# Turning keys and probabilities on VectorE as 4-byte blocks in a decode attention kernel

## The chip, the core and the metric

The kernel runs on one core of a Trainium2 chip. A core has TensorE (PE, matrix products into PSUM), VectorE (DVE), ScalarE (ACT), GpSimd (POOL) and SyncE (SP, which here issues nearly all transfers), and 16 DMA engines that carry data between HBM and SBUF. The metric is the time of one execution on the device in microseconds. A profiled execution also has a span, the time from the first to the last recorded instruction.

## The reference

One decode step of a layer: the input is normalised, one branch is attention over the last 2048 positions of a key and value cache, the other a gated unit that ends in a gate; the result is `x + s * silu(b)`. Cut to what matters:

```python
B, Sq, D = 8, 1, 512
Hq, Hkv, Sk, Dh = 32, 8, 8192, 128
W = min(4096, max(256, Sk // 4))               # 2048
xn = _layernorm(x)
q = (xn @ wq).reshape(B, Sq, Hq, Dh)...
k = jnp.repeat(k_cache[:, :, Sk - W:, :], rep, axis=1)     # rep = 4
v = jnp.repeat(v_cache[:, :, Sk - W:, :], rep, axis=1)
p = _softmax(einsum("bhqd,bhkd->bhqk", q, k) * Dh ** -0.5)
s = einsum("bhqk,bhkd->bhqd", p, v)... @ wo
h = sigmoid(xn @ w_gate) * (xn @ w_up)         # F = 1792
return x + s * silu(h @ w_down)
```

All inputs are bf16. The two caches' windows are 32 MB each, so 64 of the 81 MB that the kernel reads.

## The kernel before, in words

A *tile* here is the pair (b, i): one of 8 batch rows and one of `NQ` = 2 groups of `G` = 4 key heads. Its keys and its values are one load of 2 MB each, `k_sb` and `v_sb`, with 128 partitions of 64 positions (`CT`) times 128 elements. Partition p holds 64 consecutive positions of head p // 32. There are 16 tiles.

Loads are listed in `todo` and issued in that order on SP (`pump`, L111): a load is issued when a buffer of its tag is free (`room`, 5 buffers of tag "k" and 4 of tag "v"), and a load that has to wait holds up all loads behind it. The order is the weights of the gated unit, wq, w_down, then keys with values three tiles behind (`AHEAD`), then the 32 rows per partition of wo in five loads of tag "k". `wd_part` (L185 to 200) holds the first `SD` = 2 of the 14 rows per partition of w_down, dealt to a few partitions by `SHARES` = ((0, 5, 4), (32, 4, 3)): partitions from 0 on, 4 x 5 of them with 4 shares each, and from 32 on, 4 x 4 with 3 each. `sel_part` and `hP_sb` bring the hidden values into the same order.

Keys come with positions on partitions, but the score product needs the head dimension there. `k_transposes` (L482) turns a quarter of a tile: 16 PE transposes of 128x128 (matmuls against `perm`) into PSUM, `kT_ps`, and one DVE copy of 2048 columns to SBUF, `kT_sb`. `scores` (L498) then makes four matmuls, one per head, each on 32 columns of PE; `qm_sb` is padded with zeros so that the heads of both tiles and all quarters of one batch row b add up in one PSUM tile `s_ps` of 128 rows and 512 columns.

Softmax is per batch row: `row_max` (DVE, 512 columns), `stat_rows` (a PE transpose, `top` and `neg` on DVE, which join the row maxima of the quarters), `spread_max` (a PE transpose back, an ACT copy `nb`, four exponentials on ACT that write the rows of each head into `p_buf`, where the places of the other heads were zeroed once by POOL). `p_transposes` (16 PE transposes against `turn_rows`, one DVE copy) makes `pT_sb`. `values` makes 64 matmuls per batch row in 32-column parts of PE, each 128x256; half of each result is unwanted, and `combine` (ACT, then DVE) picks with `own_col`. `normalise` (`heads`, `divide`) and `sums` divide by the sums of the exponentials into `oP_sb`.

The loop over b (L689) spreads these steps over 16 places by hand: in the time of row b's key transposes stand the softmax of b-1 and the values of b-2. There is no scheduler; the program order on each engine is the order of the code. After the loop (L716 to 745) the last two rows are interleaved by hand.

The end (L747 on): rows 0 to 19 of wo go into `part_ps`, an ACT copy gives `part`; `fin_ps` takes `part` by way of `sel_z` first and then rows 20 to 31; `prod` and `y_bf` on DVE; one store. The gate (`w_ps`, `b_ps`, `gg_sb`, L389 to 421) is computed before the loop.

Of the kernel before, what the change touches and what calls it, by code (L numbers as in the profile page):

```python
# [10 lines left out]
def kernel(  # L11
# [31 lines left out]
    CH = CU // 2  # L43
    NU = NQ * NJ
    NR = NU * rep
# [9 lines left out]

    padpool = ctx.enter_context(tc.tile_pool(name="padpool", bufs=1))
# [3 lines left out]
    ktpool = ctx.enter_context(tc.tile_pool(name="ktpool", bufs=3))  # L60
    ppool = ctx.enter_context(tc.tile_pool(name="ppool", bufs=2))
# [23 lines left out]
    room = {"k": 5, "v": 4, "d": 1}  # L85
# [85 lines left out]
    SD = 2  # L171
    SHARES = ((0, 5, 4), (Z, 4, 3))
# [40 lines left out]
    for t0, t1 in ((0, 12), (12, KS), (KS, 26), (26, 30), (30, RT)):  # L213
        want_rows("wo_sb", A_wo, "k", RT, t0, t1)

    pump()

    perm = consts.tile([P, P], bf16, name="perm")
    nc.gpsimd.tensor_copy(
        out=perm[:].rearrange("k (l p) -> k l p", l=G),  # L220
        in_=ident[:].rearrange("k (p l) -> k l p", l=G),
    )

# [34 lines left out]
    M0 = Z - rep  # L258
    qm_sb = work.tile([P, B, Hkv, M0 + Z], bf16, name="qm_sb")
    nc.gpsimd.memzero(qm_sb[:])  # L260
    p_buf = [work.tile([P, PG, G, CU], bf16, name=f"p_buf{i}") for i in range(2)]
    for t in p_buf:
        nc.gpsimd.memzero(t[:])
# [74 lines left out]
    JQ = NB  # L338
    q_ps = [ps_s.tile([P, rep * Dh], f32, name="q_ps", tag="s") for _ in range(2)]
    for kt in range(KT):  # L340
        for x in range(Hkv // JQ):
            for j in range(JQ):
                g = x * JQ + j
                nc.tensor.matmul(  # L344
                    q_ps[x][Z * j : Z * (j + 1), :],
                    lhsT=xnT_sb[:, kt, :],
                    rhs=weights[("wq_sb", kt)][:, g * rep * Dh : (g + 1) * rep * Dh],
                    start=(kt == 0),
                    stop=(kt == KT - 1),
                    tile_position=(0, Z * j),  # L350
                    skip_group_check=True,
                )
    q_bf = ktpool.tile([P, 2, rep, Dh], bf16, name="q_bf", tag="kT")
    qT_ps = ps_t.tile([P, 2, rep, P], bf16, name="qT_ps", tag="t")
    for x in range(Hkv // JQ):
        src = q_ps[x][:].rearrange("k (r d) -> k r d", r=rep)
        nc.scalar.copy(out=q_bf[:, x], in_=src)
    for x in range(Hkv // JQ):
        for r in range(rep):
            nc.tensor.transpose(  # L360
                out=qT_ps[:, x, r, :], in_=q_bf[:, x, r, :], identity=ident[:]
            )
        nc.vector.tensor_copy(  # L363
            out=qm_sb[:, :, x * JQ : (x + 1) * JQ, M0 : M0 + rep],
            in_=qT_ps[:, x].rearrange("d r (j z) -> d z j r", z=Z)[:, ::S],
        )

    free("k")
    free("k")

    down = [(hT_sb[:, t, :], weights[("wd_sb", t)]) for t in range(SD, FT)]
# [12 lines left out]
    for x in range(SX):  # L384
        top = max(p0 + 4 * a for p0, a, sx in SHARES if x < sx)
        down += [
            (hP_sb[:top, x, Z * r : Z * (r + 1)], d_part[:top, x, r, :])
            for r in range(SD)
        ]  # L389


    w_ps = ps_s.tile([P, D], f32, name="w_ps", tag="s")
    for t, (h, w) in enumerate(down):
        j = t % NB
        nc.tensor.matmul(
            w_ps[Z * j : Z * (j + 1), :],
            lhsT=h,
            rhs=w,
            start=(t < NB),
            stop=(t >= len(down) - NB),  # L400
            tile_position=(0, Z * j),
            skip_group_check=True,
        )
    w_sb = ktpool.tile([P, 2, 512], f32, name="w_sb", tag="kT")
    nc.scalar.copy(out=w_sb[:, 0], in_=w_ps[:])
    b_ps = ps_s.tile([P, P], f32, name="b_ps", tag="s")
    for j in range(NB):
        nc.tensor.matmul(
            b_ps[Z * j : Z * (j + 1), :],
            lhsT=sel_z,  # L410
            rhs=w_sb[:, 0, j * P : (j + 1) * P],
            start=True,
            stop=True,
            tile_position=(0, Z * j),
            skip_group_check=True,
        )
    sigb = work.tile([P, P], f32, name="sigb")
    nc.scalar.activation(out=sigb[:], in_=b_ps[:], func=AF.Sigmoid)
    free("v")
    gg_sb = work.tile([P, P], f32, name="gg_sb")  # L420
    nc.vector.tensor_tensor(out=gg_sb[:], in0=sigb[:], in1=b_ps[:], op=ALU.mult)

    Hh = G * rep
    turn_rows = consts.tile([P, P], bf16, name="turn_rows")
    sel_den = consts.tile([P, Hq], f32, name="sel_den")
    sel_out = consts.tile([P, 2, Hq], f32, name="sel_out")
    for i in range(NQ):
        nc.gpsimd.tensor_copy(
            out=turn_rows[:].rearrange("k (i j l r) -> k i j l r", i=NQ, j=NJ, l=G)[
                :, i  # L430
            ],
            in_=ident[:].rearrange("k (l j i r) -> k i j l r", i=NQ, j=NJ, l=G)[:, i],
        )
        nc.vector.reduce_sum(
            out=sel_den[:, i * Hh : (i + 1) * Hh].rearrange("k (l r) -> k l r", l=G),
            in_=ident_f[:].rearrange("k (l j i r) -> k i l r j", l=G, j=NJ, i=NQ)[:, i],
            axis=AX.X,
        )
    for e in range(2):
# [19 lines left out]
    sel_sum = consts.tile([P, Hq, NDQ], f32, name="sel_sum")  # L459
    nc.gpsimd.tensor_copy(  # L460
        out=sel_sum[:], in_=sel_den[:].unsqueeze(2).to_broadcast([P, Hq, NDQ])
    )


    o_ps = ps_o.tile([P, 2, 2 * Dh], f32, name="o_ps")
# [5 lines left out]
    kT_ps = {}  # L471
# [10 lines left out]
    def k_transposes(b, u, h):  # L482
        i, j = u // NJ, u % NJ
        k_sb = k_tiles[(b, i)]
        if h == 0:
            kT_ps[0] = ps_t.tile([P, CU, P], bf16, name="kT_ps", tag="t")
        for c in range(h * CH, (h + 1) * CH):
            nc.tensor.transpose(  # L488
                out=kT_ps[0][:, c, :], in_=k_sb[:, j * CU + c, :], identity=perm[:]
            )  # L490
        if h == 1:
            kT[(b, u)] = ktpool.tile([P, CU, P], bf16, name="kT_sb", tag="kT")
            nc.vector.tensor_copy(out=kT[(b, u)][:], in_=kT_ps.pop(0)[:])  # L493
        if j == NJ - 1 and h == 1:
            del k_tiles[(b, i)]
            free("k")

    def scores(b, u):  # L498
        i, j = u // NJ, u % NJ
        if u == 0:  # L500
            s_ps[b] = ps_s.tile([P, CU * PG], f32, name="s_ps", tag="s")
        t = kT.pop((b, u))
        o = M0 - rep * (j * NQ + i)
        for l in range(G):
            nc.tensor.matmul(  # L505
                s_ps[b][NR * l : NR * (l + 1), :],
                lhsT=qm_sb[:, b, i * G + l, o : o + Z],
                rhs=t[:, :, PG * l : PG * (l + 1)],
                start=(u == 0),
                stop=(u == NU - 1),  # L510
                tile_position=(0, NR * l),
                skip_group_check=True,
            )


    NH = NQ * rep

    def row_max(b):
        st[b] = small.tile([P, 1], f32, name="st")
        nc.vector.reduce_max(out=st[b][:], in_=s_ps[b][:], axis=AX.X)  # L520

    def stat_rows(b):
        nc.tensor.transpose(out=r_ps[b % 2], in_=st.pop(b)[:], identity=ident_f[:])
        top = small.tile([1, G, NH], f32, name="top")
        nc.vector.reduce_max(
            out=top[:],
            in_=r_ps[b % 2].rearrange("o (l j h) -> o l h j", l=G, j=NJ),
            axis=AX.X,
        )
        row[b] = small.tile([1, G, NJ, NH], f32, name="neg")  # L530
        nc.vector.tensor_scalar(
            out=row[b][:],
            in0=top[:].unsqueeze(2).to_broadcast([1, G, NJ, NH]),
            scalar1=-scale,
            scalar2=None,
            op0=ALU.mult,
        )

    def spread_max(b):
        nc.tensor.transpose(  # L540
            out=nb_ps[b % 2],
            in_=row.pop(b)[:].rearrange("o l j h -> o (l j h)"),
            identity=ident_f[0:1, 0:1],
        )
        nb = small.tile([P, 1], f32, name="nb")
        nc.scalar.copy(out=nb[:], in_=nb_ps[b % 2])  # L546

        s = s_ps.pop(b)
        if b % 2 == 0:
            sums_of[b // 2] = small.tile([P, 2], f32, name="sums")  # L550
        if b == B - 1:
# [37 lines left out]
    def p_copy(b, c0, c1, copy):  # L589
        copy(out=pT[b][:, c0:c1, :], in_=pT_ps[b][:, c0:c1, :])  # L590
        if c1 == CU:
            del pT_ps[b]
# [227 lines left out]
```

## Time and profile before

| | |
|---|---|
| time, median of 3 runs | 199.51 us (199.36 to 199.6) |
| profiled execution | 199.11 us, span 197.3 us |
| busy: PE / weight loads / DVE / ACT / POOL | 155.2 / 105.4 / 114.9 / 35.8 / 13.8 us |
| instructions | 4706, of them 2138 matmuls and 2138 weight loads |
| DMA | 81.32 MB in 6436 packets, mean 412 GB/s |
| granted TensorE clock, mean | 0.972 |
| key transposes on PE (1024) | 76.5 us |
| copies of the turned keys on DVE (64) | 78.2 us |

The page lists busy time per engine, then the span in 40 slices with a digit for the busy tenths, then DMA queues, then the chain of work that ended last, then groups of instructions: line, engine, operation, tiles written and read, shape, count, then busy time, mean of one in ns, then the idle time of the engine just before them and what ended it. In a table of stretches each row has the length, the busy time and count of each engine, granted clock, DMA share and GB/s. In a chain or a timeline each row starts with start and length in us. In the slices of a chosen stretch the stretch is again cut in 40.

### The profile page before, as it was taken

The numbers are of one execution on the slowest core, as the hardware profiler recorded it, in microseconds if no ns is written. First come the engines' busy times: TensorE is split into PE (matmuls) and PEld (weight loads), VectorE is DVE, ScalarE is ACT, GpSimd is POOL, SyncE is SP. The second block draws the span as 40 slices with busy tenths as digits, with TensorE's granted clock in tenths as the row PEclk, the third lists the DMA queues.
The fourth block names the chain that finished last, engine by engine and source line by source line (L and its number), as shares of the span: only waits on it lengthen the run. The fifth ranks groups of instructions, "written<-read, shape, count | busy, mean of one in ns | idle before, by whom it ended". The sixth has DMA issues, their size and how long they took to land.

```text
span 197.3 us, 4706 instructions
## 1 busy us (share of the span) xinstructions
PE 155.2 (79%) x2138; PEld 105.4 (53%) x2138; DVE 114.9 (58%) x144; ACT 35.8 (18%) x87; POOL 13.8 (7%) x32
## 2 busy tenths in 40 slices
PE   0073575999799996999798979796989797749763
PEld 0021124777586675667565746474658464538521
DVE  4624002889877574657794766476848664764311
ACT  0510210000900600060006001500050024032110
POOL 8960001000000000000000000000000000010000
PEclk9999999999999998899999999999999999999975
DMA  6999999999999999999999999999999999999980
GB/s 212 436 438 438 423 431 422 432 435 425 428 428 435 423 428 428 442 422 425 425 432 423 432 432 425 435 428 428 432 428 425 425 428 432 438 428 424 407 372 29
DMA packets 6436, 81.32 MB, mean 412 GB/s; under 512 B 777, under 2 KB 785, under 8 KB 1553
## 3 DMA queue, kind: packets, MB, share of 16 engines
q1 hardware_dynamic: 6237, 80.10, 95.3%
q10 hardware_dynamic: 180, 0.93, 1.4%
q8 instruction: 16, 0.26, 0.5%
q14 instruction: 3, 0.02, 0.0%
HBM read 81.02 MB, written 0.01 MB: 411 GB/s over the span
## 4 chain that ended last, share of the span: by engine, by line
DMA 75%; PE 20%; SPq 1%; DVE 1%; issue 0%; ACT 0%; DVEq 0%
DMA k_sb<-in_A_k_cache_dram 62%; PE kT_ps L488 11%; DMA wo_sb<-in_A_wo_dram 10%; PE o_ps L625 4%; DMA wg_sb<-in_B_w_gate_dram 3%; PE s_ps L505 3%; PE fin_ps L768 1%; PE pT_ps L599 1%; SPq L90 1%; DVE kT_sb L493 1%; PE part_ps L754 1%; ACT part L764 0%; SPq L100 0%; SPq L150 0%; DVE prod L783 0%
## 5 line engine op out<-in xcount | busy, mean ns | idle before, releaser
L493 DVE COPY kT_sb<-kT_ps 128x2048 bf16<-128x2048 bf16 x64 | 78.2, 1222 | 37.0 <-PE kT_ps L488 36.6
L488 PE MATMUL kT_ps<-perm,k_sb 128*128 128x128 bf16 x1024 | 76.5, 225 | 12.3 <-DMA k_sb<-in_A_k_cache_dram 12.2
L488 PEld LDWEIGHTS <-k_sb 128*128 128x128 bf16 x1024 | 60.5, 100 | 32.5 <-issue 16.3
L625 PE MATMUL o_ps<-v_sb,pT_sb 128*32 128x256 bf16 x512 | 38.7, 276 | 2.3 <-DVE pT_sb L590 2.3
L625 PEld LDWEIGHTS <-pT_sb 128*32 128x32 bf16 x512 | 21.6, 96 | 10.8 <-DVE pT_sb L590 2.7
L505 PE MATMUL s_ps<-kT_sb,qm_sb 128*32 128x512 bf16 x256 | 25.9, 393 | 1.4 <-DVE kT_sb L493 1.2
L573 ACT ACTIVATE p_buf<-s_ps,nb 32x512 bf16<-32x512 f32 x28 | 19.0, 679 | 0.5
L546 ACT COPY nb<-m_ps 128x1 f32<-128x1 f32 x8 | 1.3, 159 | 91.9 <-PE m_ps L540 91.9
L590 DVE COPY pT_sb<-pT_ps 128x2048 bf16<-128x2048 bf16 (+1 forms) x8 | 9.3, 1158 | 5.0 <-PE pT_ps L599 5.0
L505 PEld LDWEIGHTS <-qm_sb 128*32 128x32 bf16 x256 | 7.4, 93 | 8.3 <-issue 1.9
L599 PE MATMUL pT_ps<-turn_rows,p_buf 128*128 128x128 bf16 x128 | 9.9, 229 | 1.1 <-ACT p_buf L573 1.1
L569 POOL COPY p_buf<-e_sb 32x512 bf16<-32x512 bf16 x1 | 0.7, 667 | 143.1 <-ACT e_sb L553 143.1
L599 PEld LDWEIGHTS <-p_buf 128*128 128x128 bf16 x128 | 8.8, 150 | 3.0 <-issue 1.6
L641 ACT ACTIVATE o_odd<-o_ps,own_col 128x128 f32<-128x128 f32 x8 | 2.9, 367 | 29.6 <-PE o_ps L625 29.6
L248 PE MATMUL xnT_ps<-ident,xn_bf 8*128 8x8 bf16 x4 | 0.3, 174 | 10.1 <-DVE xn_bf L237 10.1
L344 PE MATMUL q_ps<-wq_sb,xnT_sb 128*32 128x512 bf16 x32 | 3.8, 625 | 5.7 <-DMA wq_sb<-in_A_wq_dram 5.7
L520 DVE TENSOR_REDUCE st<-s_ps 128x1 f32<-128x512 f32 x8 | 5.4, 680 | 0.5 <-PE s_ps L505 0.5
L248 PEld LDWEIGHTS <-xn_bf 8*128 8x128 bf16 x4 | 0.2, 114 | 10.1 <-DVE xn_bf L237 10.1
L344 PEld LDWEIGHTS <-xnT_sb 128*32 128x32 bf16 x32 | 1.3, 130 | 8.1 <-issue 8.1
L363 DVE COPY qm_sb<-qT_ps 128x128 bf16<-128x128 bf16 x2 | 0.6, 292 | 8.2 <-PE qT_ps L360 8.2
L674 DVE SCALAR_TENSOR_TENSOR own<-m_ps,inv,own_q 128x128 f32<-128x128 f32 x8 | 2.8, 347 | 4.2 <-PE m_ps L664 4.2
L573 ACT ACTIVATION_READ_ACCUMULATOR p_buf<-s_ps,nb 32x1 f32 x28 | 5.1, 184 | 0.0
(86 smaller groups left out, 76.5 us busy)
## 6 DMA issues: line engine op xcount, KB each, us to landing
k_sb<-in_A_k_cache_dram SPq DMA_DIRECT2D x16, 2048.0 KB, 31.2
v_sb<-in_A_v_cache_dram SPq DMA_DIRECT2D x16, 2048.0 KB, 27.3
wq_sb<-in_A_wq_dram SPq DMA_DIRECT2D x2, 2048.0 KB, 16.7
wu_sb<-in_B_w_up_dram SPq DMA_DIRECT2D x1, 1792.0 KB, 10.2
wd_sb<-in_B_w_down_dram SPq DMA_DIRECT2D x1, 1536.0 KB
wo_sb<-in_A_wo_dram SPq DMA_DIRECT2D x1, 1536.0 KB, 18.3
wo_sb<-in_A_wo_dram SPq DMA_DIRECT2D x1, 1024.0 KB
wg_sb<-in_B_w_gate_dram ACTq DMA_DIRECT2D x1, 896.0 KB
```

The lines of the kernel that those rows point to most:

```text
L90: q0.dma_start(out=t[:].rearrange("p c d -> p (c d)"), in_=cache[b, G * i : G * (i + 1), win0:Sk, :].rearrange("l (p c) d -> p l (c d)", c ...
L344: nc.tensor.matmul(q_ps[x][Z * j : Z * (j + 1), :], lhsT=xnT_sb[:, kt, :], rhs=weights[("wq_sb", kt)][:, g * rep * Dh : (g + 1) * rep * Dh ...
L488: nc.tensor.transpose(out=kT_ps[0][:, c, :], in_=k_sb[:, j * CU + c, :], identity=perm[:])
L493: nc.vector.tensor_copy(out=kT[(b, u)][:], in_=kT_ps.pop(0)[:])
L505: nc.tensor.matmul(s_ps[b][NR * l : NR * (l + 1), :], lhsT=qm_sb[:, b, i * G + l, o : o + Z], rhs=t[:, :, PG * l : PG * (l + 1)], start=(u ...
L520: nc.vector.reduce_max(out=st[b][:], in_=s_ps[b][:], axis=AX.X)
L573: nc.scalar.activation(out=p_buf[b % 2][rows, :, l, :], in_=s[rows, :].rearrange("k (c p) -> k p c", p=PG), func=AF.Exp, bias=nb[rows, :], ...
L590: copy(out=pT[b][:, c0:c1, :], in_=pT_ps[b][:, c0:c1, :])
L599: nc.tensor.transpose(out=pT_ps[b][:, c, :], in_=p_buf[b % 2][:, :, :, c].rearrange("k p l -> k (p l)"), identity=turn_rows[:],)
L625: nc.tensor.matmul(o_at[b][rows].rearrange("k (e d) -> k e d", e=2), lhsT=pT[b][:, c, rows], rhs=v[:, m, c], start=(c == 0), stop=(c == CU ...
L641: nc.scalar.mul(out=o_odd[:], in_=o_at[b][:, Dh:], mul=own_col[:, 1:2])
L674: nc.vector.scalar_tensor_tensor(out=own[:], in0=m_ps[:, b % 2, P : 2 * P].rearrange("p (q t) -> p q t", q=NDQ), scalar=inv[b // 2][:, b % ...
```

## The change

- Keys are turned on DVE. `turn_keys` issues one 32x32-block transpose over half a key tile, read as 4-byte words (two neighbouring bf16 elements are one word): 2048 words per partition, SBUF to SBUF. A block turn stays inside 32 partitions, that is, inside one head. The PE transposes, `perm`, `kT_ps` and the PSUM copies go.
- After such a turn each partition quadrant holds the 32 words of one head's elements, and the two elements of a word lie side by side. So `scores` makes, per half tile, eight matmuls of 512 columns with the full 128 columns of PE: two halves `e` of 16 positions, times four quarters `y` of the head dimension, whose key elements are read with a step of two. `qm_sb` is laid out anew for it (spread queries, 32 short matmuls, four moves on ACT and four on DVE). One further matmul per half with 4 contracted rows (`mask_rows`, `mask_cols`) adds minus a large number to the places where a row of one head meets the keys of another.
- Softmax is per tile (16 times) instead of per batch row (8 times): `row_max` over 1024 columns, and one exponential of 128x1024 for all heads; the masked places become zero by themselves. `p_buf` needs no zeroing.
- The probabilities are turned on DVE too, 512 words per partition (`turn_p`); `pT_sb` is read by `values` as weights with a step of two elements.
- `combine` is one DVE product; `heads` adds its two halves in two matmuls. `sums` takes two matmuls.
- The loop runs over the 16 tiles, staggered: the turn of t, the softmax of t-1, the turn of the probabilities of t-2, the values of t-4. The gate's end is placed behind the scores of the first tile.
- Key buffers 4 instead of 5, `pT_sb` buffers 3 instead of 2; the last wo load takes a buffer of tag "v".
- `SD` = 1 and `SHARES` = ((0, 5, 6), (32, 2, 1)): one row per partition of w_down instead of two is dealt out.
- At the end `sel_z` stands behind the fifth of the rows of wo that go into `fin_ps`, not ahead of the first.
- The PE's instruction list is 2031 rows instead of 4205, DVE's 134 instead of 107.

```diff
-    kpool = ctx.enter_context(tc.tile_pool(name="kpool", bufs=5))
+    kpool = ctx.enter_context(tc.tile_pool(name="kpool", bufs=4))
...
-    ppool = ctx.enter_context(tc.tile_pool(name="ppool", bufs=2))
+    ppool = ctx.enter_context(tc.tile_pool(name="ppool", bufs=3))
...
-    room = {"k": 5, "v": 4, "d": 1}
+    room = {"k": 4, "v": 4, "d": 1}
...
-    SD = 2
-    SHARES = ((0, 5, 4), (Z, 4, 3))
+    SD = 1
+    SHARES = ((0, 5, 6), (Z, 2, 1))
...
+    def turn_keys(t, m):
+        k_sb = k_tiles[order[t]]
+        kT[(t, m)] = ktpool.tile([P, NJE // NE, CM, PG, NE], bf16, name="kT_sb", tag="kT")
+        nc.vector.transpose(
+            out=kT[(t, m)][:].rearrange("k y c p e -> k c y (p e)").bitcast(f32),
+            in_=k_sb[:, CM * m : CM * (m + 1), :]
+            .rearrange("k c (y d) -> k c y d", y=NJE // NE).bitcast(f32),
+        )
...
+    def scores(t, m):
...
+        nc.tensor.matmul(
+            s_ps[t][:, m],
+            lhsT=mask_rows[:].rearrange("k x l r -> k (x l r)"),
+            rhs=mask_cols[:].rearrange("k c l -> k (c l)"),
+            start=True,
+            stop=False,
+        )
+        keys = kT.pop((t, m))
+        for e in range(2):
+            for y in range(NJE):
+                nc.tensor.matmul(
+                    s_ps[t][:, m],
+                    lhsT=qm_sb[i][:, y, b, GR * (1 - e) : GR * (1 - e) + P],
+                    rhs=keys[:, y // NE, CU * e : CU * (e + 1), :, y % NE],
+                    start=False,
+                    stop=(e == 1 and y == NJE - 1),
+                )
...
+    def turn_p(t):
+        pT[t] = ppool.tile([P, NM * CU // 2, NX, 2], bf16, name="pT_sb")
+        nc.vector.transpose(
+            out=pT[t][:].rearrange("k c x e -> k (c x e)").bitcast(f32),
+            in_=p_buf[t % 2][:].rearrange("k c p e -> k (c p e)").bitcast(f32),
+        )
...
+    for t in range(NT):
+        turn_keys(t, 0)
+        if t >= 1:
+            row_max(t - 1)
+        if t >= 2:
+            turn_p(t - 2)
+        if t >= LAG:
+            values(t - LAG)
+        if t >= 1:
+            stat_rows(t - 1)
+        turn_keys(t, 1)
+        scores(t, 0)
+        if t >= 1:
+            spread_max(t - 1)
+        scores(t, 1)
+        if t == 0:
+            gg_sb = gate()
+        if t >= LAG and t % 2 == 1:
+            combine((t - LAG) // 2)
+        if t >= 8 and t % 4 == 0:
+            normalise((t - 8) // 2, (t - 8) // 2 + 2)
+        if t >= 5 and t % 4 == 1:
+            sums((t - 5) // 4)
...
     for t in range(KS, RT):
-        if t == KS:
-            into_blocks(sel_z, part[:, 0, :], True, False)
-        into_blocks(oP_sb[:, t, :], weights[("wo_sb", t)], False, t == RT - 1)
+        into_blocks(oP_sb[:, t, :], weights[("wo_sb", t)], t == KS, t == RT - 1)
+        if t == KS + 4:
+            into_blocks(sel_z, part[:, 0, :], False, False)
```

More of the change, by code (lines that the diff above doesn't have):

```diff
@@ L383 @@
     nc.scalar.copy(out=hP_sb[:], in_=hP_ps[:])
[L384 to L425, printed above, removed]
[L426 to L438 removed]
+    sel_den = consts.tile([P, GR], f32, name="sel_den")
+    sel_out = consts.tile([P, 2, Hq], f32, name="sel_out")
+    nc.vector.reduce_sum(
+        out=sel_den[:],
+        in_=ident_f[:].rearrange("k (x h) -> k h x", h=GR),
+        axis=AX.X,
+    )
     for e in range(2):
```

458 lines of the change are left out of this document (224 added, 234 removed).

## The prediction

> **What bounds the kernel now.** I read the page's busy shares and slices first, then the DMA queues and the chain, then the table of stretches.
>
> ```profile
> PE 155.2 (79%) x2138; PEld 105.4 (53%) x2138; DVE 114.9 (58%) x144; ACT 35.8 (18%) x87; POOL 13.8 (7%) x32
> DMA  6999999999999999999999999999999999999980
> q8 instruction: 16, 0.26, 0.5%
> DMA k_sb<-in_A_k_cache_dram 62%; PE kT_ps L488 11%; DMA wo_sb<-in_A_wo_dram 10%; PE o_ps L625 4%; DMA wg_sb<-in_B_w_gate_dram 3%; PE s_ps L505 3%; PE fin_ps L768 1%; PE pT_ps L599 1%; SPq L90 1%; DVE kT_sb L493 1%; PE part_ps L754 1%; ACT part L764 0%; SPq L100 0%; SPq L150 0%; DVE prod L783 0%
> ```
>
> ```profile
> 0.00:32.00 32.00, 12.41 (x108) 4.34 (x108) 9.96 (x16) 5.71 (x9) 12.67 (x30) 1.00 0.95 399
> 86.00:125.00 39.00, 35.13 (x503) 24.16 (x500) 27.01 (x32) 8.94 (x26) 0.00 (x0) 1.00 1.01 428
> 125.00:164.00 39.00, 34.27 (x488) 23.73 (x488) 25.80 (x31) 7.32 (x22) 0.00 (x0) 1.00 1.01 429
> 184.00:189.00 5.00, 3.12 (x44) 2.28 (x48) 1.93 (x6) 0.37 (x1) 0.00 (x0) 1.00 0.99 413
> 189.00:194.00 5.00, 3.90 (x76) 1.89 (x68) 0.02 (x1) 0.58 (x1) 0.00 (x0) 0.56 0.64 259
> ```
>
> The columns after the length are busy time of PE, PEld, DVE, ACT and POOL, then granted clock, DMA share, GB/s. The 16 DMA engines are full (1.01) from start to 189 us, while PE (34 to 35 of 39 us) and DVE (26 to 27) have room. The kernel is bound by bytes. Two places are left where time can move: the last stretch, where the share is 0.64, and the engine work that must stay under the transfers.
>
> The chain in order of time gives the pace:
>
> ```profile
> 7.59 24.67 DMA k_sb<-in_A_k_cache_dram
> ...
> 92.98 32.31 DMA k_sb<-in_A_k_cache_dram
> ...
> 131.47 32.73 DMA k_sb<-in_A_k_cache_dram
> ...
> 169.75 20.05 DMA wo_sb<-in_A_wo_dram
> ```
>
> The first key tile lands at 7.59 + 24.67 = 32.3 us, the 12th at 125.3, the 16th at 164.2: (164.2 - 125.3) / 4 = 9.73 us for one key and one value tile (4.87 each). Behind the last key tile only value tiles 12 to 15 and wo are queued, so the last value tile lands near 164.2 + 4 x 4.87 = 183.7.
>
> **The change, part by part.** *Engine work per tile, which must fit in 9.73 us.* The rows I price it from:
>
> ```profile
> L493 DVE COPY kT_sb<-kT_ps 128x2048 bf16<-128x2048 bf16 x64 | 78.2, 1222 | 37.0 <-PE kT_ps L488 36.6
> L590 DVE COPY pT_sb<-pT_ps 128x1024 bf16<-128x1024 bf16 x1 | 0.7, 692 | 2.3 <-PE pT_ps L599 2.3
> L573 ACT ACTIVATE p_buf<-s_ps,nb 32x512 bf16<-32x512 f32 x28 | 19.0, 679 | 0.5
> L520 DVE TENSOR_REDUCE st<-s_ps 128x1 f32<-128x512 f32 x8 | 5.4, 680 | 0.5 <-PE s_ps L505 0.5
> L683 DVE TENSOR_REDUCE oP_sb<-own 128x32 bf16<-128x128 f32 x8 | 3.1, 387 | 0.3
> L674 DVE SCALAR_TENSOR_TENSOR own<-m_ps,inv,own_q 128x128 f32<-128x128 f32 x8 | 2.8, 347 | 4.2 <-PE m_ps L664 4.2
> L525 DVE TENSOR_REDUCE top<-m_ps 1x32 f32<-1x128 f32 x8 | 2.2, 276 | 0.8 <-PE m_ps L523 0.5
> L531 DVE TENSOR_SCALAR neg<-top 1x128 f32<-1x128 f32 x8 | 1.7, 215 | 0.3
> L333 DVE STREAM_TRANSPOSE hT_sb<-h_sb 128x448 bf16<-128x448 bf16 x1 | 0.6, 645 | 0.0
> ```
>
> Removed: 64 PE transposes and four PSUM copies per key tile, 1024 and 64 in all (78.2 us of DVE), and the PE transposes of the probabilities. Added: two VectorE turns of 2048 four-byte words per key tile, and one of 512 words for its probabilities. No row has a 4-byte turn. The copies of 2048 and 1024 columns (1222 and 692 ns) differ by 0.52 ns a column over a fixed 162; with that fixed part the one turn here, 645 ns for 448 two-byte elements, took 1.08 ns an element. So 2048 words take 0.16 + 2.21 = 2.37 us and 512 take 0.71, if a word costs what an element did. Ends: 1.2 us, if words moved like the copy's columns; 4.6 us, if each word went as two elements. I take 2.37, the row of the same instruction.
>
> DVE per tile: turns 2 x 2.37 = 4.74; maximum over 1024 instead of 512 columns, 0.68 + 0.52 (the 680 ns less 162, once more) = 1.20; probabilities 0.71; top 0.28; neg 0.22; half a combine, now one step over 256 elements, (0.35 + 0.13) / 2 = 0.24; half of a normalisation, (0.35 + 0.39) / 2 = 0.37; some eight gaps of 0.04 = 0.3. Together 8.1 us. Before it was 25.8 to 27.0 per 39 us, so 6.5 to 6.8 per tile: DVE becomes the fullest engine, still 1.6 us under the pace. On DVE the first turn of tile t+1, the next maximum and the probabilities stand behind the second turn of t, and `top` waits for a PE transpose that stands behind 9 score matmuls and 32 value matmuls.
>
> That PE stretch, from these rows:
>
> ```profile
> 130.78 1.07 PE L488 MATMUL kT_ps<-perm,k_sb 128*128 128x128 bf16 x16
> ...
> 184.59 1.92 PE L625 MATMUL o_ps<-v_sb,pT_sb 128*32 128x256 bf16 x32
> ```
>
> Sixteen 128-column matmuls take 1.07 us, so 512 columns cost 0.27 and nine of them 2.4; 32 value matmuls 1.9. PE is through 4.3 us after a second turn ends, DVE needs about 0.6 (combine, normalise) + 2.37 + 1.20 + 0.71 = 4.9 there: the wait is nothing, or 0.3 us where no combine falls. PE holds 18 x 0.27 + 1.9 + 0.5 = 7.3 us per tile. ACT: one exponential of 1024 columns per tile, 0.68 + 0.52 and a short read, about 1.4 us, where four of 0.68 stood per two tiles. All of this is costed at nothing, because 9.73 us of transfer lie over 8.1 to 8.4. If that cover went, each 0.1 us too much per tile would cost up to 1.5 us.
>
> *Start.*
>
> ```profile
> 21.59 1.90 PE L344 MATMUL q_ps<-wq_sb,xnT_sb 128*32 128x512 bf16 x16 [2.95 <-DMA wq_sb<-in_A_wq_dram]
> ```
>
> The queries are spread by ACT and DVE copies of 2048 columns (about 2.3 us), 32 short matmuls and four moves on each engine, about 8 us from the last query matmul (23.5 us): ready near 31.4, under the first key tile's 32.3. The gate then sits between the turns of tiles 0 and 1 on DVE (about 3 us waiting). Tiles 0 to 3 arrive 4.9 us apart, faster than 8; DVE catches up by tile 8. POOL's `perm` copy and `p_buf` zeroing go, unseen: nothing on the chain waits for POOL.
>
> *Queue.* Key buffers fall from 5 to 4. Between the landings of key tiles t and t+4 lie 38.9 us; the slot is free after about 8, the transfer needs 4.9: 26 us to spare. On SP each load stands behind the slot wait of the one before; the value slot for tile t comes free in the same iteration, earlier. The fifth wo load takes a value slot, freed by tile 12 soon after 169, more than ten us before its turn.
>
> *End.* The last matmuls:
>
> ```profile
> 189.84 1.04 PE L754 MATMUL part_ps<-wo_sb,oP_sb 128*32 128x512 bf16 x8 [0.30 <-DMA wo_sb<-in_A_wo_dram]
> ...
> 191.57 0.66 PE L768 MATMUL fin_ps<-part,sel_z 128*32 128x128 f32 x8 [0.69 <-ACT part L764]
> ...
> 192.00 1.93 PE L768 MATMUL fin_ps<-wo_sb,oP_sb 128*32 128x128 bf16 x48
> 193.53 0.13 PEld L768 LDWEIGHTS <-oP_sb 128*32 128x32 bf16 x7 [0.20 <-issue]
> 193.98 0.29 DVE L783 TENSOR_TENSOR prod<-gg_sb,fin_ps 128x128 f32<-128x128 f32 x1 [5.32 <-PE fin_ps L768]
> ```
>
> Moving `sel_z` behind five rows hides the ACT copy, but the same 56 matmuls (0.66 + 1.93) remain behind the third wo load, which lands about when they started. I take nothing for it; the end follows the wo landings.
>
> *Bytes and their spread, the only term of the sum.* The output needs the slowest DMA engine. The DMA share in slices of 0.15 us from 188 us on, and the two loads that even the engines out:
>
> ```profile
> DMA  7969694997997977977788787776656632000000
> ```
>
> ```profile
> wd_part<-in_B_w_down_dram SPq DMA_DIRECT2D x1, 160.0 KB
> wd_part<-in_B_w_down_dram SPq DMA_DIRECT2D x1, 96.0 KB
> ```
>
> The share fades from about 190.4 and is zero from the 35th slice, 193.1; the last matmuls start at 193.53. So engines end up to 2.7 us apart. In the last stretch 0.64 of 5 us is 3.2 us of full work, which spread evenly would end at 192.2: even spread is worth 0.9. Instruction fetches: 16 packets, 0.5% of 16 x 197.3 us = 15.8, so 0.99 us of one engine each. PE's list falls from 4205 rows to 2031, so about 8 fetches go: 0.5 us averaged over 16 engines. `wd_part`, read as `a` engines per share, puts 32 + 24 KB on four engines and 32 KB on one, at 428 / 16 = 26.8 GB/s 2.1 and 1.2 us; afterwards 24 to 28 KB, 1.05 us at most, and every engine 8 KB more, 0.3. The views don't show which engines fetch. If both surpluses halve (two fetches on an engine become one), the 2.7 falls by about 1.35, less the 0.3: 1.0. Ends: 0, where a fetch and a share meet on one engine (0.99 + 1.05 is the old 2.1), and 0.9 + 0.5 = 1.4, where all end together. I take 0.9, beside the halving and a little below it, since the shares needn't sit on the engines without fetches.
>
> Sum: the profiled execution took 199.11 (span 197.3 and 1.8 around it); 199.11 - 0.9 = 198.2. The median of the runs is 0.4 above, 199.51, so 198.6.
>
> **Rules weighed.** Granted clock was 1.00 with PE 3.12 of 5 us busy and 0.56 in the stretch where PE waits for wo. The Trainium skill (TensorE: Matmul & The Clock Gate, "Why this matters for your kernels") says that idle gaps over about 3 us halve the clock; the new loop leaves PE two gaps of about 1.3 and 2 us per tile, so by that rule it stays fast, but narrowly. The same skill (Vector Engine (DVE) Microarchitecture Reference, 3.8) states one element per cycle per lane for the turn, without a width; by it a key turn would be near the 2.37 us above, and no run so far shows one at 4 bytes.
>
> **Rivals.** (1) Slower: a 4-byte turn takes two cycles a word. The loop becomes 8.1 + 2 x 2.2 = 12.5 us; from 32.3, 15 x 12.5 + 17 for the last tile's chain + 9 for values, heads and wo + 2.7 to the end + 1.8 around = 250. It decides from about 2.9 us a turn: tile 15 must start by about 166 for its probabilities to be turned when the last values land (183.7), which 9.2 us per tile still gives. For it: no 4-byte row. Against: same instruction, one stream.
>
> (2) Slower: PE's reads, now 4 bytes apart, or a halved clock hold the loop.
>
> ```profile
> L488 PEld LDWEIGHTS <-k_sb 128*128 128x128 bf16 x1024 | 60.5, 100 | 32.5 <-issue 16.3 <-DMA k_sb<-in_A_k_cache_dram 15.2
> L599 PEld LDWEIGHTS <-p_buf 128*128 128x128 bf16 x128 | 8.8, 150 | 3.0 <-issue 1.6 <-ACT p_buf L573 1.4
> ```
>
> A 32-byte step made weight loads 1.5 times as long. At 1.5 a half tile's scores take 3.5 us, the loop about 9.0, no loss; at 2 (or half clock) 10 to 12, 213 to 243. Against: 4 bytes is a small step.
>
> (3) No gain: shares and fetches meet on one engine, 199.1 to 199.9.
>
> (4) Slightly slower: the last tile's chain (17 us from its landing at 164.2, slack 2.5) ends behind wo: 200 to 201.
>
> **The numbers.** Forecast 0.68, (1) 0.10, (2) 0.07, (3) 0.10, (4) 0.05. 0.2% is 0.4 us, what a measurement can tell. Faster 0.68, same 0.10, slower 0.22. The forecast's own range is 198.1 to 199.1 (the bounds of the 0.9, cut at the 0.2%); with a little below it for the fetches' true price, with (3) and most of (4), 0.82 lies in 197.8 to 201.0.
>
> **What would show it.** The new page: turns of 2048 words at 2.4 us, DVE near 8 of each 9.73 us and idle on key landings; DMA share 1.0 to the end, 7 to 9 instruction packets; a last stretch fuller than 0.64. Wrong if turns exceed 2.9 us, if DMA slices fall below 9 in mid-run, or if the last wo landing doesn't move.

## The result, and the profile after

The changed kernel takes 198.28 us (median of 4 runs, 198.11 to 198.4) where the kernel before takes 199.56 (199.36 to 199.77): a ratio of 0.9935, 95% interval 0.9918 to 0.9952. The profiled execution took 198.22 us with a span of 196.4; before it was 199.11 and 197.3. Of one kernel below, the one with two dealt rows, five of eleven executions took 205.0 to 218.4 us for a reason that stays open, and its ratio goes by the other six.

The page of the changed kernel: busy time by engine, the DMA slices of the span, the queue of instruction packets, and the chain by engine.

```profile
PE 139.9 (71%) x1063; PEld 67.0 (34%) x1077; DVE 131.3 (67%) x144; ACT 32.4 (17%) x62; POOL 11.8 (6%) x31
DMA  5999999999999999999999999999999999999990
q8 instruction: 8, 0.13, 0.2%
DMA 49%; PE 23%; DVE 21%; ACT 2%; issue 1%; SPq 1%; DVEq 0%; ACTq 0%
```

The transfers still run without a hole. PE lost half its instructions, and the instruction packets went from 16 to 8. The chain passes through PE and VectorE for 44% of the span, so the tile loop stands near the pace of the transfers. The groups that are new, with the duration of one in ns behind the busy time:

```profile
L503 DVE STREAM_TRANSPOSE kT_sb<-k_sb 128x2048 f32<-128x2048 f32 x32 | 72.8, 2288 | 5.0 <-DMA k_sb<-in_A_k_cache_dram 4.9
L539 DVE TENSOR_REDUCE st<-s_ps 128x1 f32<-128x1024 f32 x16 | 19.1, 1192 | 4.8 <-PE s_ps L529 4.8
L571 ACT ACTIVATE p_buf<-s_ps,nb 128x1024 bf16<-128x1024 f32 x16 | 17.8, 1113 | 0.5
L582 DVE STREAM_TRANSPOSE pT_sb<-p_buf 128x512 f32<-128x512 f32 x16 | 11.1, 691 | 0.0
```

The table of stretches of the changed kernel, in the columns of the prediction (PE, PEld, DVE, ACT, POOL, granted clock, DMA share, GB/s):

```profile
86.00:125.00 39.00, 31.72 (x218) 15.55 (x222) 29.03 (x32) 6.79 (x15) 0.00 (x0) 0.89 1.01 431
125.00:164.00 39.00, 30.46 (x208) 14.76 (x210) 27.59 (x31) 4.13 (x10) 0.00 (x0) 0.85 1.01 430
189.00:194.00 5.00, 2.87 (x64) 1.68 (x63) 0.58 (x2) 0.59 (x1) 0.00 (x0) 0.60 0.50 202
```

Here the clock fell to 0.85 to 0.89 where it had been 1.00, and the last stretch has less to move (0.50), not more. The end in the timeline of the changed kernel:

```profile
190.84 0.73 PE L753 MATMUL fin_ps<-wo_sb,oP_sb 128*32 128x128 bf16 x20 [1.22 <-DMA wo_sb<-in_A_wo_dram]
191.34 0.65 PE L753 MATMUL fin_ps<-part,sel_z 128*32 128x128 f32 x8
191.77 1.34 PE L753 MATMUL fin_ps<-wo_sb,oP_sb 128*32 128x128 bf16 x28
192.71 0.14 PEld L753 LDWEIGHTS <-oP_sb 128*32 128x32 bf16 x7 [0.21 <-issue]
193.16 0.29 DVE L768 TENSOR_TENSOR prod<-gg_sb,fin_ps 128x128 f32<-128x128 f32 x1 [6.33 <-PE fin_ps L753]
```

`prod` starts at 193.16 instead of 193.98, 0.82 earlier; the span is 0.9 shorter. The gain of this pair is in when the last rows of wo land: the last of the five loads lands at 193.5 in the kernel before (issued at 171.2, 22.3 us to landing) and at 192.7 in the changed one (176.4 and 16.3), and the weight loads for the last matmuls start at 193.53 and 192.71. The rate in slices of 0.15 us from 188 us on, first of the kernel before:

```profile
GB/s 314 532 287 519 287 642 178 560 437 314 478 464 328 423 300 328 382 328 328 301 355 328 300 328 287 314 300 232 246 232 259 246 123 82 0 0 0 0 0 0
DMA packets 452, 1.70 MB, mean 284 GB/s; under 512 B 59, under 2 KB 59, under 8 KB 416
```

and of the changed kernel:

```profile
GB/s 287 478 533 178 587 410 300 573 314 369 573 259 396 423 369 382 382 355 355 341 300 273 287 259 178 109 96 55 14 0 0 0 0 0 0 0 0 0 0 0
DMA packets 410, 1.42 MB, mean 236 GB/s; under 512 B 53, under 2 KB 53, under 8 KB 406
```

Such rows give two numbers for every run below, each from one execution. *Left* is what is still to move at 188 us: 1.70 and 1.42 MB, which at 428 GB/s would end at 191.97 and 191.32 if all engines ended together. *Last* is the end of the last slice that is not zero: 193.1 (34th) and 192.35 (29th). The *excess*, last less even end, is read here as how far the slowest DMA engine stands behind the mean: 1.1 and 1.0. So in this pair 0.65 of the 0.75 us came from less being left at 188 us, and only 0.1 from a narrower spread. Of the 0.28 MB less, 0.13 are the eight packets (81.32 MB against 81.19 in all); the rest had moved earlier (431 and 430 GB/s from 86 to 164 us, where it was 428 and 429), and why is not shown.

### The profile page after: what moved, and what is told of

It is laid out like the page before. It is cut to its first block, busy times and chain, and to the rows that moved or that the text cites. A ratio compares the mean times of both kernels' runs of the same rounds, so it can differ in the third digit from the quotient of the medians.

```text
span 196.4 us, 2531 instructions
## 1 busy us (share of the span) xinstructions
PE 139.9 (71%) x1063; PEld 67.0 (34%) x1077; DVE 131.3 (67%) x144; ACT 32.4 (17%) x62; POOL 11.8 (6%) x31
## 2 busy tenths in 40 slices
DMA packets 6426, 81.19 MB, mean 413 GB/s; under 512 B 775, under 2 KB 911, under 8 KB 1551
## 4 chain that ended last, share of the span: by engine, by line
DMA 49%; PE 23%; DVE 21%; ACT 2%; issue 1%; SPq 1%; DVEq 0%; ACTq 0%
DMA k_sb<-in_A_k_cache_dram 29%; PE s_ps L529 14%; DVE kT_sb L503 13%; DMA wo_sb<-in_A_wo_dram 10%; DMA wq_sb<-in_A_wq_dram 10%; DVE st L539 4%; PE s_ps L519 2%; PE o_ps L606 2%; DVE qm_sb L453 1%; PE fin_ps L753 1%; ACT qm_sb L453 1%; PE q_ps L416 1%; SPq L103 1%; ACT q_bf L430 1%; DVE pT_sb L582 1%
## 5 line engine op out<-in xcount | busy, mean ns | idle before, releaser
L503 DVE STREAM_TRANSPOSE kT_sb<-k_sb 128x2048 f32<-128x2048 f32 x32 | 72.8, 2288 | 5.0 <-DMA k_sb<-in_A_k_cache_dram 4.9
L529 PE MATMUL s_ps<-kT_sb,qm_sb 128*128 128x512 bf16 x242 | 71.6, 442 | 5.9 <-DVE kT_sb L503 3.4
L529 PEld LDWEIGHTS <-qm_sb 128*128 128x128 bf16 x256 | 24.9, 105 | 43.9 <-issue 24.8
L606 PE MATMUL o_ps<-v_sb,pT_sb 128*32 128x256 bf16 x512 | 30.2, 273 | 0.0
L539 DVE TENSOR_REDUCE st<-s_ps 128x1 f32<-128x1024 f32 x16 | 19.1, 1192 | 4.8 <-PE s_ps L529 4.8
L544 PE MATMUL m_ps<-ident_f,st 128*1 128x128 f32 x16 | 4.4, 276 | 22.3 <-DVE st L539 22.3
L571 ACT ACTIVATE p_buf<-s_ps,nb 128x1024 bf16<-128x1024 f32 x16 | 17.8, 1113 | 0.5
L519 PE MATMUL s_ps<-mask_cols,mask_rows 4*128 4x512 bf16 x32 | 14.2, 445 | 0.0
L582 DVE STREAM_TRANSPOSE pT_sb<-p_buf 128x512 f32<-128x512 f32 x16 | 11.1, 691 | 0.0
L228 DVE CAST x_f<-x_bf 8x512 f32<-8x512 bf16 x1 | 5.2, 5150 | 2.5 <-DMA x_bf<-in_A_x_dram 2.5
L660 PE MATMUL m_ps<-o_sb,sel_res 128*128 128x256 f32 (+1 forms) x20 | 4.6, 352 | 1.2 <-DVE o_sb L644 0.5
```

What stands on the lines that cost most here:

```text
L228: nc.vector.tensor_copy(out=x_f[:], in_=x_bf[:])
L503: nc.vector.transpose(out=kT[(t, m)][:] .rearrange("k y c p e -> k c y (p e)") .bitcast(f32), in_=k_sb[:, CM * m : CM * (m + 1), :] .rearr ...
L519: nc.tensor.matmul(s_ps[t][:, m], lhsT=mask_rows[:].rearrange("k x l r -> k (x l r)"), rhs=mask_cols[:].rearrange("k c l -> k (c l)"), sta ...
L529: nc.tensor.matmul(s_ps[t][:, m], lhsT=qm_sb[i][:, y, b, GR * (1 - e) : GR * (1 - e) + P], rhs=keys[:, y // NE, CU * e : CU * (e + 1), :, ...
L539: nc.vector.reduce_max(out=st[t][:], in_=s_ps[t][:].rearrange("k m c -> k (m c)"), axis=AX.X)
L544: nc.tensor.transpose(out=r_ps[t % 2], in_=st.pop(t)[:], identity=ident_f[:])
```

## The experiments

Each run stands against runs of the kernel before on the same chip (their medians 199.26 to 199.48).

**The changed kernel again.**

> The changed kernel again, beside the next three on the same chip. Both theories: 198.3 us, 1.3 under the kernel before.

Measured: 198.06 us (197.98 to 198.24), ratio 0.9935 (0.9923 to 0.9946). The gain is 1.3 us, and the kernel before varies more (199.05 to 199.85 in all but three of 29 runs) than the changed one does.

**Two dealt rows again, on the changed kernel.** The shares of `wd_part` amount to 256 KB as before, in loads of 120, 96 and 40 KB (the zeroing of its buffer on POOL is widened to match).

```diff
-    SD = 1
-    SHARES = ((0, 5, 6), (Z, 2, 1))
+    SD = 2
+    SHARES = ((0, 5, 3), (Z, 4, 3), (2 * Z, 5, 1))
```

> The changed kernel with the old deal of w_down: two rows per partition, 56 KB more on four DMA engines and 32 KB more on one (written in three shares so that it fits, the same bytes per engine as before the change). Theory S (the gain is the slowest DMA engine's: fewer instruction fetches and the new deal together): 8 instruction packets as in the changed kernel, but the engines with shares end some 1.0 us later and all engines 0.3 sooner, so the end moves to about 199.0 (198.6 to 199.2). Rival E (the gain is from the engines' work or the order of the last matmuls): 198.3, as the changed kernel.

Measured: ratio 1.0016 (1.0002 to 1.0029), about 199.8 us. The whole gain is gone though VectorE still turns the keys and the packets are 8. The queue row, and the rate from 188 us on:

```profile
q8 instruction: 8, 0.13, 0.2%
GB/s 464 423 437 382 369 382 355 451 492 314 382 546 300 437 451 260 478 451 300 437 396 341 396 259 328 355 300 273 246 178 164 137 137 96 68 27 55 55 27 14
DMA packets 466, 1.79 MB, mean 299 GB/s; under 512 B 60, under 2 KB 60, under 8 KB 428
```

The even end is 192.18, and the tail ends with the last of these slices, at 194.0 (in the 2 us behind it nothing moves): the excess is 1.8 us, against 1.0. The larger rest (1.79 MB) is another 0.9 us, and about 0.8 of it was lost earlier in this execution, between 20 and 36 us, where this kernel moved less than the 428 GB/s of the kernel before:

```profile
20.00:36.00 16.00, 6.80 (x72) 2.71 (x69) 7.89 (x7) 4.76 (x6) 0.00 (x0) 1.00 1.01 406
```

What caused that stretch is not settled: the third load of `wd_part` also made SP issue the first key tile at 8.79 us instead of 7.72. So only about half of the loss can be put down to the spread. The expectation of a loss held; the size, 1.7 us above the changed kernel, was more than twice the 0.7 expected.

**The new shares alone, on the kernel before.**

```diff
-    SD = 2
-    SHARES = ((0, 5, 4), (Z, 4, 3))
+    SD = 1
+    SHARES = ((0, 5, 6), (Z, 2, 1))
```

> The kernel before with the new deal of w_down alone (one row per partition, shares 5 x 6 and 2 x 1). Theory S: 16 instruction packets stay, engines with two fetches are the last ones and get 0.3 us of w_down more: 199.6 to 199.9, no gain. Rival D (the deal alone makes the gain): 198.6 to 198.9.

Measured: 200.02 us, ratio 1.0028 (0.9999 to 1.0057). With 16 packets the new deal gains nothing:

```profile
q8 instruction: 16, 0.26, 0.5%
GB/s 532 232 587 451 396 423 410 369 369 382 396 382 355 410 396 328 328 451 314 314 396 273 287 287 246 259 246 232 191 219 205 191 191 137 68 41 27 14 0 0
DMA packets 449, 1.70 MB, mean 283 GB/s; under 512 B 57, under 2 KB 57, under 8 KB 415
```

The rest at 188 us is that of the kernel before to the second digit (1.70 MB), but it ends at 193.7: excess 1.7 instead of 1.1. This execution did not end on that tail alone:

```profile
191.87 1.26 PE L754 MATMUL part_ps<-wo_sb,oP_sb 128*32 128x512 bf16 x20 [0.86 <-DVE oP_sb L683]
194.06 0.85 PE L768 MATMUL fin_ps<-wo_sb,oP_sb 128*32 128x128 bf16 x48
```

The matmuls into `part_ps` wait for `oP_sb` until 191.87, where they began at 188.71 before, and the last 48 run without a wait, since the last load (172.0 + 22.0) has landed. So 16 packets with 256 KB dealt out, and 8 with 128 KB, are the pairings with the smaller excess; each crossed pairing has 1.7 or more and no gain, but part of either loss has another source.

**More instruction packets.** Mask matmuls of 16 columns are added behind the one of 512 (they only lower scores that are masked already), so that PE's list grows while the transfers and VectorE's work stay.

```diff
+        for _ in range(7):
+            nc.tensor.matmul(
+                s_ps[t][:, m, :16],
+                lhsT=mask_rows[:].rearrange("k x l r -> k (x l r)"),
+                rhs=mask_cols[:].rearrange("k c l -> k (c l)")[:, :16],
+                start=False,
+                stop=False,
+            )
```

> The changed kernel with 7 more matmuls of 16 columns per half tile, which add the mask once more on 16 columns (224 matmuls and 224 weight loads: PE's list 2479 rows instead of 2031). Theory S: 9 to 10 instruction packets instead of 8, one or two DMA engines fetch twice and end last: 198.8 to 199.3. Rival E: PE has some 8 of 39 us free and the additions take about 0.7 us per tile: 198.3, unchanged.

Measured: 199.07 us (198.79 to 199.7), ratio 0.9984 (0.9972 to 0.9996): 1.0 us of the gain is given back. The list has 2479 rows:

```profile
q8 instruction: 10, 0.16, 0.3%
GB/s 218 560 355 396 478 382 328 587 314 423 478 328 382 478 382 314 410 341 314 369 328 273 287 164 273 137 109 82 41 27 27 27 27 27 14 27 14 0 0 0
DMA packets 415, 1.46 MB, mean 243 GB/s; under 512 B 54, under 2 KB 54, under 8 KB 406
193.25 0.41 PE L761 MATMUL fin_ps<-wo_sb,oP_sb 128*32 128x128 bf16 x16 [0.48 <-DMA wo_sb<-in_A_wo_dram]
193.87 0.29 PE L761 MATMUL fin_ps<-wo_sb,oP_sb 128*32 128x128 bf16 x8 [0.22 <-DMA wo_sb<-in_A_wo_dram]
```

The rest at 188 us is hardly larger (1.46 MB), but a tail at 27 GB/s, the rate of one engine (428 / 16 = 26.8), runs on to 193.55: excess 2.1. That reads as one engine being last, and the last matmuls wait for the landings, as expected. The tenth packet is itself fetched late, between 191.5 and 192 us, so in this kernel a late fetch could cost as much as one too many.

With four and with fourteen of these matmuls, on the kernel with earlier matmuls that is described below (198.04 us with 8 packets):

> The kernel with the earlier matmuls (198.04 us, 8 instruction packets) with four more 16-column mask matmuls per half tile, which add nothing new to the scores: PE's list grows from 2031 to 2287 rows, so by one instruction packet, to 9. If a packet costs what it holds up its own DMA engine, one engine has one packet more and all loads wait for that engine: 198.6 to 199.1. If packets cost only their share of the total transfer work (0.99 us over 16 engines each): 198.1, no change that can be seen.

> As the kernel before it in this list, with fourteen more mask matmuls per half: PE's list has 2927 rows, 11 or 12 instruction packets. If the slowest DMA engine counts and the added packets go to different engines: 199.0 to 199.4, about what two added packets gave (199.07 with 10 packets), since no engine has more than one packet above the rest. If each packet costs about 0.5 us, as the step from 8 to 10 would also allow: 199.8 to 200.2. If only the total work counts: 198.3.

Measured: 199.12 us (198.78 to 199.25) with four, 199.29 (199.03 to 199.38) with fourteen. The lists have 2287 and 2927 rows; the queue rows, one fence for each:

```profile
q8 instruction: 9, 0.15, 0.3%
```

```profile
q8 instruction: 12, 0.20, 0.4%
```

| packets | 8 | 9 | 10 | 12 | 16 (kernel before) |
|---|---|---|---|---|---|
| time, us | 198.04 | 199.12 | 199.07 | 199.29 | 199.26 to 199.48 |
| ratio to before | 0.9936 | 0.9975 | 0.9984 | 0.9985 | 1 |
| left at 188 us, MB | 1.39 | 1.44 | 1.46 | 1.52 | 1.70 |
| excess, us | 0.95 | 1.4 | 2.1 | 1.7 | 1.1 |

The ninth packet costs most of what ten cost: 0.8 us by the ratios, 1.1 by the times (the kernels with 8 and with 9 ran on different chips); from nine to twelve it is 0.2 more. The excess of single executions (198.78 us with nine, 199.35 with ten) should not be ranked. The cost is not PE's added work, since fourteen matmuls cost hardly more than four, and not the lateness of a fetch, since with nine packets the last one is fetched between 186 and 187 us, as with eight. It fits the slowest engine, not the sum of the work: one packet too many on one engine delays every load, and further packets on other engines cost their share of the total, about 0.08 us each ((1.52 - 1.39) / 0.428 / 4). No view shows the engines one by one. The nine-packet time lies just above the top of its expected range, the twelve-packet time within its range for the slowest engine.

**All engines the same share.** Eight groups of partitions with 4 shares each instead of five with 6 and two with 1.

```diff
-    SHARES = ((0, 5, 6), (Z, 2, 1))
+    SHARES = ((0, 8, 4),)
```

> The changed kernel with the one dealt row of w_down on eight engines, 16 KB each (one share, 8 x 4), instead of 24 to 28 KB on five. Theory S: the engines that end last carry a share and an 8 KB fetch; their share falls by 0.3 to 0.45 us. If the three further engines are those that fetch nothing: 197.8 to 198.1. If they also fetch: 198.4 to 198.7. Rival E (the deal is of no account): 198.3.

Measured: 198.4 us (198.22 to 198.53), ratio 0.9945 (0.9925 to 0.9966). No gain: the expected 197.8 to 198.1 was missed, and 198.4 lies in the second range, 0.1 from the rival's time, so the two are not told apart. (A fetch is 16 KB, 0.13 MB in 8 packets, not 8.) Left 1.39 MB, last slice 192.2, excess 0.95, about as in the changed kernel. What remains is not in how 128 KB are dealt.

**`sel_z` first again.**

```diff
-        into_blocks(oP_sb[:, t, :], weights[("wo_sb", t)], t == KS, t == RT - 1)
-        if t == KS + 4:
-            into_blocks(sel_z, part[:, 0, :], False, False)
+        if t == KS:
+            into_blocks(sel_z, part[:, 0, :], True, False)
+        into_blocks(oP_sb[:, t, :], weights[("wo_sb", t)], False, t == RT - 1)
```

> The changed kernel with the old order at the end: sel_z ahead of the rows of wo in the last product. Theory S (the end follows the landings of wo, the order is worth nothing): 198.3 us, within 0.2 of the changed kernel. Rival E (hiding the ACT copy of 0.59 us is part of the gain): 198.7 to 198.9.

Measured: 198.03 us (197.97 to 198.35), ratio 0.993 (0.9909 to 0.995). The order at the end is worth nothing.

**How thick the cover is.** The turn of the probabilities of tiles 0 to 11 is issued twice, then four times, which adds 0.69 and 2.07 us of VectorE to each of these tiles.

```diff
-        nc.vector.transpose(
+        for _ in range(2 if t < 12 else 1):
+            nc.vector.transpose(
```

> The changed kernel with the turn of the probabilities made twice for tiles 0 to 11 (the same result written again): 0.69 us more of DVE per tile. Theory S (DVE's loop of about 7.7 us is hidden under 9.73 us of transfer): 198.3, unchanged to 0.2. Rival D (DVE already sets the pace): 12 x 0.69 = 8 us more, at least 200.

Measured: 198.15 us (198.04 to 198.21): hidden.

> The same with the turn made four times for tiles 0 to 11: 2.07 us more of DVE per tile, so about 9.8 us where a transfer pair takes 9.73. Theory S: the cover is gone, the last tile is turned 5 to 10 us late and the end moves with it: 202 to 208. If a loop on DVE is hidden however long: 198.3.

Measured: 216.98 us (214.58 to 217.45), ratio 1.0843 (1.0792 to 1.0895). The direction was right, the size was not: 18.9 us instead of 4 to 10. The second turns of tiles 1 and 15 start at 45.38 and 192.63, so the loop took 147.3 us. With 8.1 + 2.07 us for twelve iterations and 8.1 for two it would have been 138. VectorE's waits in the changed kernel show what the 8.1 lacked (total, times, longest, in us):

```profile
DVE inv L598 <- PE m_ps L590: 9.8, 3, 4.4
DVE own L670 <- PE m_ps L660: 8.8, 4, 4.2
DVE kT_sb L503 <- DMA k_sb<-in_A_k_cache_dram: 4.9, 3, 2.6
DVE st L539 <- PE s_ps L529: 4.8, 4, 1.8
```

In two of every four tiles VectorE ends an iteration with a normalisation or with the reciprocal of the sums, and waits up to 4.4 us for PE matmuls that stand behind both halves' scores. The same in the kernel with four turns, first the waits, then one case in the timeline:

```profile
DVE own L671 <- PE m_ps L661: 10.4, 4, 4.5
DVE st L539 <- PE s_ps L529: 8.1, 6, 2.4
DVE inv L599 <- PE m_ps L591: 7.7, 3, 3.4
119.56 3.47 PE L529 MATMUL s_ps<-kT_sb,qm_sb 128*128 128x512 bf16 x8 [1.76 <-DVE kT_sb L503]
124.01 0.35 DVE L671 SCALAR_TENSOR_TENSOR own<-m_ps,inv,own_q 128x128 f32<-128x128 f32 x1 [4.50 <-PE m_ps L661]
```

Two causes were to be told apart: the place of these matmuls in PE's order, and the slower PE clock (eight score matmuls took 3.47 us, at full clock 1.97). So the matmuls were issued earlier, ahead of both halves' scores, with four turns and with one (`sums_mm` and `sums_inv` are the two parts of `sums`).

```diff
             stat_rows(t - 1)
+        if t >= 8 and t % 4 == 0:
+            heads((t - 8) // 2, (t - 8) // 2 + 2)
+        if t >= 5 and t % 4 == 1:
+            sums_mm((t - 5) // 4)
         turn_keys(t, 1)
...
-            normalise((t - 8) // 2, (t - 8) // 2 + 2)
+            divide((t - 8) // 2)
+            divide((t - 8) // 2 + 1)
...
-            sums((t - 5) // 4)
+            sums_inv((t - 5) // 4)
```

> As x8 (the probabilities of tiles 0 to 11 are turned four times, 2.07 us more of VectorE per tile), with one move: the PE matmuls of a normalisation and of the sums are issued right after the row statistics, ahead of the second turn of the tile, and only VectorE's reading of them stays at the end of the iteration. In x8 VectorE waited 4.4 to 4.5 us for these matmuls, which stood behind both halves' scores, in two of every four tiles, about 2.2 us per tile. Theory A (these waits are the excess of the loop over 8.1 + 2.07 us): the waits go, the loop comes to about 9.9 to 10.3 us per tile, 203 to 210 us. Theory B (the halved PE clock alone makes the scores, and so everything behind them, late): the waits turn up at another instruction, 213 to 218 us. For each, the wait rows of VectorE on the normalisation and the sums tell whether they went.

Measured: 210.07 us (208.09 to 210.75), ratio 1.0526 (1.0457 to 1.0596). The waits of this kernel:

```profile
DVE st L539 <- PE s_ps L529: 5.9, 6, 1.8
DVE own L677 <- ACT nb L568: 5.5, 3, 2.8
DVE inv L605 <- ACT nb L568: 5.4, 3, 2.8
DVE own L677 <- PE m_ps L667: 1.6, 2, 0.8
```

These four sum to 18.4 us; the three above, with four turns and the old order, to 26.2. About 8 us of waiting went, and the span fell by 7.2 (215.0 to 207.8). So the place of the matmuls is a cause, as theory A says, though 210.07 is just above its range: the move took only part of the wait, since VectorE's reading now waits, by the profile, for the ACT copy `nb`, which stands behind the first half's scores. How much of the rest is the clock's stays open.

> The changed kernel with the same move (matmuls of normalisation and sums ahead of the second turn) and no doubled turn. Under A and B alike the engine work stays under the transfers, so 198.0 to 198.4 us; but A says that the last key tile's first turn starts nearer to its landing (164.5 against 163.4 in the changed kernel; with the move at most 0.6 us behind) and that VectorE waits longer for key landings in mid-run, that is, the cover becomes thicker by about 2 us per tile.

Measured: 198.04 us (197.95 to 198.16), ratio 0.9936 (0.992 to 0.9952): no gain in time, as expected, but more cover. VectorE waits for keys

```profile
DVE kT_sb L503 <- DMA k_sb<-in_A_k_cache_dram: 16.5, 8, 3.1
163.21 2.31 DVE L503 STREAM_TRANSPOSE kT_sb<-k_sb 128x2048 f32<-128x2048 f32 x1 [3.04 <-DMA k_sb<-in_A_k_cache_dram]
```

16.5 us instead of 4.9, and the last tile's first turn now waits for its landing at 163.2, where it started at 164.5 in the changed kernel. That is 0.8 us more cover per tile (11.6 / 14), where 2 had been expected.

## Why the prediction was right

The kernel became faster, by 1.3 us where 0.9 was forecast; 198.28 and 198.06 us lie 0.3 and 0.5 below the 198.6, the second just outside the forecast's own range (198.1 to 199.1).

*What bounds it.* Right. The DMA share is 1.01 in mid-run in both kernels, and no change of engine work that stayed under the pace (one turn more, `sel_z`, earlier matmuls) moved the time.

*The turns.* Right: 2.29 and 0.69 us against 2.37 and 0.71; the maximum 1.19 against 1.20, the exponential 1.11 + 0.19. The two turns differ by 1.04 ns a word ((2288 - 691) / 1536), what an element of 2 bytes cost before (1.08). Both ends of the range, 1.2 and 4.6 us, were far off. The Trainium skill (Vector Engine (DVE) Microarchitecture Reference, 3.8) states one element per cycle per lane for the transpose, without a width; the two rows fit it if a 4-byte word is the element, since a word took no longer than 2 bytes did.

*The tile loop.* Near in its sum, wrong in its parts. Busy time is 29.03 per 39 us, 7.2 us per tile, less than the 7.8 that the steps came to without the gaps. But "the wait is nothing, or 0.3 us" holds only for the step that was examined, `top` behind the scores and values:

```profile
DVE top L546 <- PE m_ps L544: 1.4, 6, 0.4
```

The waits for PE in the normalisations and sums were not on the list and amount to 18.6 us (9.8 + 8.8). From the second turn of tile 1 to that of tile 15 the changed kernel needs 123.8 us (46.41 to 170.19); without the 4.9 on key landings that is 8.5 us per tile, not 8.1. Rival 1's threshold was rightly placed, but its sum does not close: from 32.3 to 166 in 15 steps is 8.9 us a tile, not 9.2. The runs give it. With one turn more VectorE never waits for a key landing and its second turn of tile 15 starts at 169.71 (8.8 us per tile from 45.97), hidden; with four turns it starts 22.9 us later, at 192.63, and the time is 18.8 us longer. So about 4 us were still free at 169.71, which puts the threshold near 9.1 us per tile.

*The start.* The first turn begins at 32.38 right behind the queries, about 1 us later than "near 31.4", so no slack was left. The gate's wait was 5.1 us instead of 3. Neither cost anything: VectorE first waits for a landing at tile 8, as forecast:

```profile
95.42 2.31 DVE L503 STREAM_TRANSPOSE kT_sb<-k_sb 128x2048 f32<-128x2048 f32 x1 [1.22 <-DMA k_sb<-in_A_k_cache_dram]
```

*The end.* Right: the order of `sel_z` is worth nothing (198.03 with the old one).

*The rule on the clock.* "It stays fast, but narrowly" was wrong. In the timeline of the changed kernel:

```profile
129.05 1.74 PE L529 MATMUL s_ps<-kT_sb,qm_sb 128*128 128x512 bf16 x7 [0.17 <-issue]
137.81 0.27 PE L544 MATMUL m_ps<-ident_f,st 128*1 128x128 f32 x1 [2.59 <-DVE st L539]
138.57 2.95 PE L529 MATMUL s_ps<-kT_sb,qm_sb 128*128 128x512 bf16 x7 [0.17 <-issue]
161.33 0.27 PE L544 MATMUL m_ps<-ident_f,st 128*1 128x128 f32 x1 [1.80 <-DVE st L539]
162.08 2.61 PE L529 MATMUL s_ps<-kT_sb,qm_sb 128*128 128x512 bf16 x7 [0.17 <-issue]
```

In mid-run PE's gaps ahead of `m_ps` went up to 3.1 us, not 1.3 and 2, because VectorE came late. Seven matmuls took 2.95 us behind a gap of 2.59 and 2.61 behind one of 1.80, instead of 1.74; the granted clock was 0.54 and 0.62 while they ran. Behind gaps of up to 1.43 us they ran at full speed in this execution. The Trainium skill's rule (TensorE: Matmul & The Clock Gate, "Why this matters for your kernels", gaps over about 3 us) named the right danger; here gaps of 2.59 and 1.80 us were enough. It cost no time: two executions of the changed kernel with a mean clock of 0.914 and 0.851 took 198.22 and 198.23 us.

*The term of the sum.* Right in size, partly by luck, and wrong in its split. For the profiled pair 0.9 was forecast and 0.9 measured. But the step "if both surpluses halve (two fetches on an engine become one), the 2.7 falls by about 1.35, less the 0.3" did not happen: the excess of the slowest engine went from 1.1 to 1.0 only, and 0.65 us came from less being left for all engines, of which the prediction had named 0.5 (8 packets of 0.99 us over 16 engines). The four pairings of packets and shares suggest why. Both kernels hold shares that fit their packets (16 with 256 KB, 8 with 128 KB), and each mixture has an excess of 1.7 or more and no gain. The likeliest reading is that shares and fetches sit on different engines, so that the old spread had been evened out already, and the new deal was needed to keep it so while the total fell. The views don't show engines by number, and both mixtures lost time elsewhere too, so this is argued from the four pairings, not seen. What is shown is that the packets matter: put back on the changed kernel, they take 0.8 to 1.0 of the 1.3 us.

*The median.* The other 0.4 us of the gain come from the last step, the 0.4 added for the median of the runs: the profiled execution of before was among its fastest, that of the changed kernel was not (198.22, beside medians of 198.28 and 198.06). Which execution was profiled is chance, not mechanism.

*"A last stretch fuller than 0.64"* was a wrong sign to look for. It came out at 0.50, because less was left at 189 us.

## What to carry to other kernels

When all DMA engines are full, the end waits for the last landing: count the instruction packets as transfers, and when their number changes, try dealing the uneven loads anew, since either alone gained nothing here. Half a list of PE instructions was worth 1.3 us only because it fell to 8 packets; with 9 the gain was 0.3 to 0.5. Cover is to be priced as the pace of the loop with every wait of the fullest engine in it, rare iterations included, not as a sum of busy times.

## What was not expected of the hardware

- The price of instruction packets is a step: 8 packets 198.04 us, 9 packets 199.12, 12 packets 199.29 (0.9936, 0.9975 and 0.9985 of the kernel before on the same chip).
- The list of 2031 rows takes 8 packets and one of 2287 takes 9, so this kernel stands less than 256 rows below a step worth 0.8 to 1.1 us.
- PE gaps of 2.59 and 1.80 us were followed by matmuls at 0.42 and 0.37 us each instead of 0.25.
